# A Fourier mixing layer with a squared-ReLU FFN: the row d = 128 spread by DMA, its multiples made by GpSimd a block ahead, and squares taken in place

## The chip, the core and the metric

The kernel runs on one core of a Trainium2 chip. The metric is the device time of one execution in microseconds. One execution was also recorded by the hardware profiler; all durations of single instructions are from that one. In what follows PE is TensorE (PEld its weight loads), DVE is VectorE, ACT is ScalarE, POOL is GpSimd and SP is SyncE, and L763 is line 763 of the kernel.

## The reference

```python
# x (8, 3008, 256), w_in (256, 2048), w_out (2048, 256), all float32
y = np.fft.fft(np.fft.fft(x, axis=1), axis=2).real.astype(np.float32)
y = y.reshape(8 * 3008, 256)
h = np.maximum(y @ w_in, 0.0)
out = (h * h @ w_out).astype(np.float32)
```

The real part of a two-dimensional Fourier transform over 3008 positions and 256 channels replaces attention; a feed-forward layer with a squared ReLU follows.

## The kernel before, in words

**What is computed where.** The transform along the channels is folded into `w_in`: a table `gh` holds it in three forms (`gh[:, 0]` for cosines, `gh[:, 1]` for sines, `gh[:, 2]` for sines with a factor of minus two). The transform along the positions gives, for each column (one frequency k of one batch), a cosine part `zc` and a sine part `zs` of 128 channels each. With P the product of the cosine table with `zc` and Q that of the sine table with `zs`, one column serves two frequencies, k and S - k: one takes P + Q, the other P - Q. So the kernel goes over some 12,000 columns, not 24,064 rows, in 25 blocks (`wins`), 0 to 24: 240, 512, 512, 240, 512 and 448 columns, then 512 each, and 360 in the last.

**A block.** Each block `w` has eight steps `s`, and each step two chunks of 128 of the 2048 hidden channels. A normal step does the following.

- `pq` (L762, L763): four matmuls of up to 512 columns, into a PSUM tile `ph` (pool `ps_h`, two buffers).
- the square of the step before (`power`, L814, on VectorE), then the ReLU of the first sign (L809, on ScalarE) into a tile `h1`, and its square from `h1` into `h2`.
- `others`: the second product of the block before (`ffn2_steps`, L665, sixteen matmuls of 256 columns a step, so 128 a block), with its evacuation on ScalarE (L680) and its output stores on the SP queue (L645); the jobs of the folds of coming batches, on VectorE and GpSimd; and a share of the z matmuls (L558) that make `zc` and `zs` of the next block.
- `turn` (L798): two matmuls more, with `gh[:, 2]`, which turn P + Q into P - Q in the same PSUM tile.
- the ReLU of the second sign. Its square comes at the next step and reads `h1` backwards, since frequency S - k counts down.

A differencing step (steps 2, 4 and 6 of a block from block 4 on, or step 5 alone in a block with a fold, listed in `diff`) saves the two matmuls of `turn`. `cosines` (L784) makes P alone; `twice` (L788, VectorE) computes t2 = n2 - 2P from PSUM; after `others`, `sines` (L793) adds Q to the same PSUM tile, so it has to wait for `twice`; one ReLU is taken on ScalarE as ever, and the other on VectorE as a saturating add of t2 and P + Q (L807).

**The row d = 128.** Row 0 of `zs` carries the channel d = 128 in the place where the sine of d = 0 would be nought. `n2` is twice its contribution N: the row spread over all partitions times a column `g2n`. Before, `spread_nyq` spreads the row in step 0 of the same block by a matmul with `sel`, a matrix of ones in its first row (L770, into a tile of the pool `ps_z`), ScalarE takes it to `zn` (L772), and `nyq_rows` multiplies it on ScalarE, two instructions for each differencing step (L778).

**The order.** The schedule is manual: each engine executes its instructions in the order in which the code issues them, and SP and GpSimd their transfers likewise. `at[s]` and `post[s]` list the jobs of the folds for each step. Block `fold_at` does the first fold of a batch, block `late_at` its late part: two `fold8` (L472) and two `fold16` (L483) on VectorE, the last with `nyq8`, small copies on GpSimd (L489 to L491). The blocks with a first fold are 5, 8, 10, 13, 16 and 19 (one differencing step each); those with a late part 6, 9, 12, 15, 18 and 21. The z matmuls of the odd frequencies (unit `e = 0`) and of the even ones (`e = 1`, which read what the late part and `nyq8` wrote) are spread over the steps `lo` to `hi`; each unit has two parts, 0 for `zc` (cosine) and 1 for `zs` (sine), and two halves `h`. After the last matmul of a part, `minus` (L581, VectorE) writes the second run of its columns.

Of the kernel before, what the change touches and what calls it, by code (L numbers as in the profile page):

```python
# [16 lines left out]
P = 128  # L17
# [12 lines left out]
def kernel(  # L30
# [76 lines left out]
    h1p = ctx.enter_context(tc.tile_pool(name="h1p", bufs=3))  # L107
    h2p = ctx.enter_context(tc.tile_pool(name="h2p", bufs=2))
    wp = ctx.enter_context(tc.tile_pool(name="wp", bufs=2))
    znp = ctx.enter_context(tc.tile_pool(name="znp", bufs=1))  # L110
# [73 lines left out]
    sel = const.tile([P, P], F16, name="sel")  # L184
    nc.gpsimd.memset(sel, 0.0)
    nc.gpsimd.memset(sel[0:1, :], 1.0)
# [350 lines left out]

    def z_steps(u, late=False):
# [15 lines left out]
        def mm(part, h, k, last, o0, o1, lhs, tab):  # L554
            if h == 0 and k == 0:
                st[part] = ps_z.tile([P, 512], F32, name="pz", tag="pz")
# [21 lines left out]
        def minus(part):  # L578
            es, ps = st["es", part], st[part]
            for w, o, a, cnt in spans(c0 + n, n2):  # L580
                nc.vector.scalar_tensor_tensor(out=zwin(w)[part][:, o : o + cnt], in0=es[:, a : a + cnt], scalar=2.0, in1=ps[:, a : a + cnt], op0=ALU.mult, op1=ALU.subtract)  # L581
# [126 lines left out]
    diff = {w: (5,) if w in fold_at else (2, 4, 6) for w in range(4, NW)}  # L708
    BIG = 3.0e38
    old = None  # L710
    for w in range(NW):
# [4 lines left out]
        lo, hi = 0, NST - 1  # L716
# [48 lines left out]
        n2s = {}  # L765
        t2s = {}

        def spread_nyq():
            pn = ps_z.tile([P, 512], F32, name="pn", tag="pz")
            nc.tensor.matmul(pn[:, 0:wn], sel, zsw[:, 0:wn], start=True, stop=True)  # L770
# [3 lines left out]
        def nyq_rows(s):  # L774
            n2 = n2s[s] = wp.tile([P, 2, WN], F32, name="n2", tag="w16")
            for a in range(2):
                fc = 2 * s + a
                nc.scalar.activation(n2[:, a, 0:wn], n2s["zn"][:, 0:wn], AF.Copy, bias=0.0, scale=g2n[:, fc : fc + 1])  # L778
# [7 lines left out]
        def twice(s):  # L786
            t2 = t2s[s] = tmp.tile([P, 3 * NE], F32, name="t2", tag="tt")[:, 0 : 2 * WN].rearrange("p (a n) -> p a n", a=2)
            nc.vector.scalar_tensor_tensor(out=t2[:, :, 0:wn], in0=phs[s][:, :, 0:wn], scalar=-2.0, in1=n2s[s][:, :, 0:wn], op0=ALU.mult, op1=ALU.add)  # L788
# [11 lines left out]
        def relu(s, sg):  # L800
            h1 = h1p.tile([P, 2, 512], F16, name="h1", tag="h1")
            if w == 1 and not sg:

                for a in range(2):
                    nc.scalar.activation(h1[:, a, 0:wn], phs[s][:, a, 0:wn], AF.Relu, bias=0.0, scale=-1.0)
            elif sg and s in t2s:
                nc.vector._custom_dve(TENSOR_ADD_SAT, out=h1[:, :, 0:wn], in0=t2s[s][:, :, 0:wn], in1=phs[s][:, :, 0:wn], s0=BIG, s1=0.0)  # L807
            else:
                nc.scalar.activation(h1[:, :, 0:wn], phs[s][:, :, 0:wn], AF.Relu, bias=0.0, scale=-1.0)  # L809
            return h1  # L810

        def power(s, sg, h1):
            hv = rev_dim(h1[:, :, 0:wn], 2) if sg else h1[:, :, 0:wn]
            nc.vector.tensor_tensor(h2[:, 2 * s : 2 * s + 2, sg * wn : (sg + 1) * wn], hv, hv, op=ALU.mult)  # L814

        def square(s, sg):
            power(s, sg, relu(s, sg))
# [14 lines left out]
        kept = None  # L832
        for s0 in range(0, NST, 2 if w == 0 else 1):
            ss = range(s0, s0 + (2 if w == 0 else 1))
            if s0 in diff.get(w, ()):
                cosines(s0)
                twice(s0)
                if kept:
                    power(*kept)
                others(s0)  # L840
                sines(s0)
                h1a = relu(s0, 0)
                h1b = relu(s0, 1)
                power(s0, 0, h1a)
                kept = (s0, 1, h1b)
            else:
                for s in ss:
                    pq(s)
                if kept:
                    power(*kept)  # L850
                for s in ss:
                    square(s, 0)
                if s0 + 1 in diff.get(w, ()):
                    nyq_rows(s0 + 1)
                for s in ss:
                    others(s)
                if s0 == 0 and w in diff:
                    spread_nyq()
                for s in ss:
                    turn(s)  # L860
                if w == 0:
                    for s in ss:
                        square(s, 1)
                    kept = None
                else:
                    kept = (s0, 1, relu(s0, 1))
        if kept:
            power(*kept)
# [35 lines left out]
```

## Time and profile before

| what | value |
|---|---|
| median of 3 runs | 641.57 us (639.27 to 641.66) |
| the profiled execution's own time | 640.49 us |
| its span, first to last instruction | 638.5 us |
| mean granted TensorE clock | 0.994 |
| TensorE busy | 603.5 us, 95% of the span |
| ScalarE busy | 476.9 us, 75% |
| VectorE busy | 472.3 us, 74% |
| GpSimd busy | 75.9 us, 12% |

A row of a group reads: line, engine, operation, output <- input by the program's names, shapes, count, then the busy time in us, the mean of one in ns, and the idle time of the engine just before, with what ended it. A row of waits reads: engine and what waited <- what ended the wait, total us, times, longest. A row of the timeline reads: start in us, duration in us, engine, line, operation, what it writes <- what it reads, shapes, how many in a row. The ends of matmuls are modelled, and their durations overlap, so the distance from one start to the next says more than the duration.

### The profile page before, as it was taken

To read this page: it belongs to the slowest core of one execution; us is meant where nothing else is said; L and a number is where in the kernel's file an instruction comes from. 1 tells how busy PE (TensorE), PEld (TensorE's weight loads), DVE (VectorE), ACT (ScalarE), POOL (GpSimd) and SP (SyncE) were. 2 spreads that over 40 slices of the span, in tenths; PEclk is the share of its full clock that TensorE was granted. 3 is DMA by queue.
4 is the path that set the end of the run, shared out by engine and by line. 5 is a ranking of instruction groups with operands and counts; after the bars stand their busy time and mean duration, and the time that the engine had idled before them with its cause. 6 is when DMAs were issued, how large, how long until landed. Compare 5 with 4: busy or idle time off the path is not lost.

```text
span 638.5 us, 11636 instructions
## 1 busy us (share of the span) xinstructions
PE 603.5 (95%) x4485; PEld 431.5 (68%) x4485; DVE 472.3 (74%) x712; ACT 476.9 (75%) x690; POOL 75.9 (12%) x134
## 2 busy tenths in 40 slices
PE   4799998799999999999999999999999999999995
PEld 2456686576677766776667776777767766677784
DVE  7777855896969868768788578877788677787660
ACT  6677767877788777787868787778777877787761
POOL 8202220012000220220003200021000200000000
PEclk9989999999999999999999999999999999999998
DMA  8736331135111731631116411173111311111121
GB/s 152 111 84 126 110 87 43 32 73 158 45 43 35 147 109 34 122 114 54 35 51 120 122 33 49 39 147 96 45 28 56 107 37 38 45 45 49 39 61 55
DMA packets 36543, 47.53 MB, mean 74 GB/s; under 512 B 4232, under 2 KB 30344, under 8 KB 36488
## 3 DMA queue, kind: packets, MB, share of 16 engines
q0 software_dynamic: 9344, 22.14, 17.1%
q1 hardware_dynamic: 26915, 24.44, 12.8%
q8 instruction: 35, 0.57, 0.4%
q10 hardware_dynamic: 228, 0.21, 0.1%
q14 instruction: 21, 0.16, 0.1%
HBM read 33.63 MB, written 27.84 MB: 96 GB/s over the span
## 4 chain that ended last, share of the span: by engine, by line
PE 70%; DVE 15%; ACT 6%; issue 4%; POOL 2%; DMA 1%; ACTq 1%; POOLq 0%; DVEq 0%
PE po L665 38%; PE ph L763 7%; PE ph L762 7%; PE ph L798 7%; DVE h L814 4%; PE ph L793 4%; DVE t L788 4%; ACT h L809 3%; DVE h L807 3%; PE pz L558 3%; PE ph L784 2%; DVE xy L472 1%; ACTq L645 1%; POOL xo L133 1%; PE pn L770 1%
## 5 line engine op out<-in xcount | busy, mean ns | idle before, releaser
L809 ACT ACTIVATE h<-ph 128x1024 f16<-128x1024 f32 (+3 forms) x341 | 315.8, 970 | 73.2 <-PE ph L793 48.4
L665 PE MATMUL po<-wout,h 128*128 128x256 f16 (+1 forms) x3024 | 362.0, 273 | 0.0
L665 PEld LDWEIGHTS <-h 128*128 128x128 f16 (+1 forms) x3024 | 296.8, 98 | 72.0 <-issue 0.6
L814 DVE TENSOR_TENSOR h<-h 128x1024 f16<-128x1024 f16 (+3 forms) x400 | 251.9, 655 | 72.7 <-ACT h L809 67.0
L762 PE MATMUL ph<-zc,gh 128*128 128x512 f16 (+3 forms) x298 | 107.7, 365 | 2.7 <-ACT h L809 1.3
L763 PE MATMUL ph<-zs,gh 128*128 128x512 f16 (+3 forms) x298 | 107.7, 365 | 0.9 <-DVE zs L581 0.7
L807 DVE CUSTOM_DVE_ANT_0 h<-t,ph 128x1024 f16<-128x1024 f32 x47 | 57.4, 1221 | 44.5 <-ACT h L809 43.4
L798 PE MATMUL ph<-zs,gh 128*128 128x512 f16 (+3 forms) x298 | 83.9, 364 | 3.8 <-ACT h L809 2.2
L680 ACT ACTIVATE osb<-po 128x512 f32<-128x512 f32 (+2 forms) x94 | 54.9, 587 | 33.6 <-PE po L665 28.7
L788 DVE SCALAR_TENSOR_TENSOR t<-ph,n 128x1024 f32<-128x1024 f32 (+2 forms) x51 | 61.1, 1199 | 14.0 <-PE ph L784 11.0
L778 ACT ACTIVATE n<-zn,g2n 128x512 f32<-128x512 f16 (+2 forms) x102 | 67.3, 717 | 0.0
L763 PEld LDWEIGHTS <-gh 128*128 128x128 f16 x298 | 29.1, 98 | 34.6 <-issue 3.6
L762 PEld LDWEIGHTS <-gh 128*128 128x128 f16 x298 | 29.1, 98 | 32.4 <-issue 2.0
L793 PE MATMUL ph<-zs,gh 128*128 128x512 f16 (+2 forms) x102 | 29.8, 373 | 10.4 <-DVE t L788 9.8
L798 PEld LDWEIGHTS <-gh 128*128 128x128 f16 x298 | 27.9, 98 | 13.1 <-issue 6.2
L784 PE MATMUL ph<-zc,gh 128*128 128x512 f16 (+2 forms) x102 | 29.9, 375 | 0.0
L772 ACT ACTIVATE zn<-pn 128x512 f16<-128x512 f32 (+2 forms) x21 | 12.4, 589 | 17.7 <-PE pn L770 17.6
L489 POOL COPY xy<-xy 128x2 f16<-128x2 f16 x16 | 2.5, 188 | 164.8 <-DVE xy L472 164.8
L793 PEld LDWEIGHTS <-gh 128*128 128x128 f16 x102 | 9.4, 97 | 16.8 <-issue 14.3
L128 POOL DMA_DIRECT2D xo<-in_x_dram x8 | 6.1, 765 | 119.5 <-DVE fo L423 109.0
L133 POOL DMA_INDIRECT xo<-in_x_dram,idx_r x15 | 18.3, 1218 | 4.5 <-issue 4.3
L784 PEld LDWEIGHTS <-gh 128*128 128x128 f16 x102 | 10.0, 98 | 11.6
(134 smaller groups left out, 344.2 us busy)
## 6 DMA issues: line engine op xcount, KB each, us to landing
out_dram<-osb SPq DMA_DIRECT2D x77, 128.0 KB
xo<-in_x_dram POOLq DMA_DIRECT2D x7, 768.0 KB, 6.7
scr<-ev POOLq DMA_DIRECT2D x8, 390.0 KB, 3.3
rb<-scr POOLq DMA_DIRECT2D x16, 130.0 KB
out_dram<-osb SPq DMA_DIRECT2D x12, 94.0 KB
w<-in_moe_w_in_dram POOLq DMA_DIRECT2D x2, 512.0 KB
wout<-in_moe_w_out_dram POOLq DMA_DIRECT2D x1, 1024.0 KB
out_dram<-osb SPq DMA_DIRECT2D x8, 75.0 KB
```

Source lines behind the costliest of these rows:

```text
L665: nc.tensor.matmul(po[0:m, j * D : (j + 1) * D], h2[:, fc, q : q + m], wout16[:, fc, :], start=(fc == 0), stop=(fc == NFC - 1))
L680: nc.scalar.activation(osb[0:mm].rearrange("p s d -> p (s d)")[:, lo:hi], po[0:mm, lo:hi], AF.Copy, bias=0.0, scale=HS * HS)
L762: nc.tensor.matmul(ph[:, a, 0:wn], gh[:, 0, f0 : f0 + P], zcw[:, 0:wn], start=True, stop=False)
L763: nc.tensor.matmul(ph[:, a, 0:wn], gh[:, 1, f0 : f0 + P], zsw[:, 0:wn], start=False, stop=True)
L778: nc.scalar.activation(n2[:, a, 0:wn], n2s["zn"][:, 0:wn], AF.Copy, bias=0.0, scale=g2n[:, fc : fc + 1])
L784: nc.tensor.matmul(ph[:, a, 0:wn], gh[:, 0, f0 : f0 + P], zcw[:, 0:wn], start=True, stop=True)
L788: nc.vector.scalar_tensor_tensor(out=t2[:, :, 0:wn], in0=phs[s][:, :, 0:wn], scalar=-2.0, in1=n2s[s][:, :, 0:wn], op0=ALU.mult, op1=ALU.add)
L793: nc.tensor.matmul(phs[s][:, a, 0:wn], gh[:, 1, f0 : f0 + P], zsw[:, 0:wn], start=False, stop=True, skip_group_check=True)
L798: nc.tensor.matmul(phs[s][:, a, 0:wn], gh[:, 2, f0 : f0 + P], zsw[:, 0:wn], start=False, stop=True, skip_group_check=True)
L807: nc.vector._custom_dve(TENSOR_ADD_SAT, out=h1[:, :, 0:wn], in0=t2s[s][:, :, 0:wn], in1=phs[s][:, :, 0:wn], s0=BIG, s1=0.0)
L809: nc.scalar.activation(h1[:, :, 0:wn], phs[s][:, :, 0:wn], AF.Relu, bias=0.0, scale=-1.0)
L814: nc.vector.tensor_tensor(h2[:, 2 * s : 2 * s + 2, sg * wn : (sg + 1) * wn], hv, hv, op=ALU.mult)
```

## The change

- The row of the next block's `zs` is written by SP to a row of DRAM and read back into all 128 partitions (`zn`), in step 6 of the block before (step 7 where the z matmuls end late). The matmul with `sel` and its copy on ScalarE go, and so does `sel`.
- The products `n2` for all differencing steps of the next block are made at once after that, on GpSimd. The pool of `n2` has three buffers, that of `zn` two.
- The ReLUs write straight into `h2`, the one of the second sign backwards; `h1` goes. One in-place square for each step, over both signs, comes one step later (after `twice`, where that next step is a differencing one); step 7's first sign is squared at once.
- The z matmuls end a step earlier in general (`hi`), and take part 1 before part 0. `minus` of a step that stands ahead of a differencing step is held until after `twice`.
- Fold jobs move: `odds` to step 5, and the late jobs to steps 2, 4, 6 and 7. Block 4 has two differencing steps, not three.

```diff
+    held = {"on": False, "jobs": []}
+    def let_go():
+        jobs, held["jobs"] = held["jobs"], []
+        for j in jobs:
+            j()
...
         def minus(part):
+            if held["on"]:
+                held["jobs"].append(lambda: apart(part))
+            else:
+                apart(part)
...
-    diff = {w: (5,) if w in fold_at else (2, 4, 6) for w in range(4, NW)}
+    diff = {w: (4, 6) if w == 4 else (5,) if w in fold_at else (2, 4, 6) for w in range(4, NW)}
...
-        lo, hi = 0, NST - 1
+        lo, hi = 0, NST - 2
...
-            at = [[f] for f in fj[0:5]] + [[], fj[6:7], fj[7:8]]
-            post[5] = fj[5:6]
+            at = [[f] for f in fj[0:4]] + [[], fj[4:5], fj[6:7], fj[7:8]]
+            post[6] = fj[5:6]
...
-                at[st + 2] = at[st + 2] + folds[late_at[w]]["late"][st : st + 1]
+                at[(2, 4, 6, 7)[st]] += folds[late_at[w]]["late"][st : st + 1]
...
-            zj += [(zu, 0, 0), (zu, 1, 0), (zu, 0, 1), (zu, 1, 1)]
+            zj += [(zu, 1, 0), (zu, 0, 0), (zu, 1, 1), (zu, 0, 1)]
...
         def spread_nyq():
-            pn = ps_z.tile([P, 512], F32, name="pn", tag="pz")
-            nc.tensor.matmul(pn[:, 0:wn], sel, zsw[:, 0:wn], start=True, stop=True)
-            zn = n2s["zn"] = znp.tile([P, WN], F16, name="zn", tag="zn")
-            nc.scalar.activation(zn[:, 0:wn], pn[:, 0:wn], AF.Copy, bias=0.0, scale=1.0)
...
-                nc.scalar.activation(n2[:, a, 0:wn], n2s["zn"][:, 0:wn], AF.Copy, bias=0.0, scale=g2n[:, fc : fc + 1])
+            wn1 = wins[w + 1][1]
+            row = drp.tile([1, WN], F16, name="row", tag="row")
+            nc.sync.dma_start(out=row[:, 0:wn1], in_=zwin(w + 1)[1][0:1, 0:wn1])
+            zn = znp.tile([P, WN], F16, name="zn", tag="zn")
+            nc.sync.dma_start(out=zn[:, 0:wn1], in_=bass.AP(tensor=row.tensor, offset=row.offset, ap=[[0, P], [1, wn1]]))
+            for s in diff[w + 1]:
+                n2 = n2s[w + 1, s] = wp.tile([P, 2, WN], F32, name="n2", tag="w16")
+                for a in range(2):
+                    fc = 2 * s + a
+                    nc.gpsimd.tensor_scalar(out=n2[:, a, 0:wn1], in0=zn[:, 0:wn1], scalar1=g2n[:, fc : fc + 1], scalar2=None, op0=ALU.mult)
...
         def relu(s, sg):
-            h1 = h1p.tile([P, 2, 512], F16, name="h1", tag="h1")
+            h = h2[:, 2 * s : 2 * s + 2, sg * wn : (sg + 1) * wn]
+            if sg:
+                h = rev_dim(h, 2)
...
-        def power(s, sg, h1):
-            hv = rev_dim(h1[:, :, 0:wn], 2) if sg else h1[:, :, 0:wn]
-            nc.vector.tensor_tensor(h2[:, 2 * s : 2 * s + 2, sg * wn : (sg + 1) * wn], hv, hv, op=ALU.mult)
+        def power(s, a, b):
+            h = h2[:, 2 * s : 2 * s + 2, a * wn : b * wn]
+            nc.vector.tensor_tensor(h, h, h, op=ALU.mult)
...
+            held["on"] = s0 + ng in diff.get(w, ())
             if s0 in diff.get(w, ()):
                 cosines(s0)
                 twice(s0)
-                if kept:
-                    power(*kept)
+                settle()
                 others(s0)
                 sines(s0)
-                h1a = relu(s0, 0)
-                h1b = relu(s0, 1)
-                power(s0, 0, h1a)
-                kept = (s0, 1, h1b)
+                relu(s0, 0)
+                relu(s0, 1)
+                kept.append((s0, 0, 2))
+                if s0 == hi and w + 1 in diff:
+                    spread_nyq()
+                continue
```

`settle` takes the squares that are kept and then calls `let_go`; in a normal step it comes right after `pq`.

More of the change, by code (lines that the diff above doesn't have):

```diff
@@ L578, in minus, with apart @@
         def minus(part):
+            if held["on"]:
+                held["jobs"].append(lambda: apart(part))
+            else:
+                apart(part)
+        def apart(part):
             es, ps = st["es", part], st[part]
@@ L830, in others, with settle @@
                     j()
-        kept = None
-        for s0 in range(0, NST, 2 if w == 0 else 1):
-            ss = range(s0, s0 + (2 if w == 0 else 1))
+        kept = []
+        def settle():
+            for k in kept:
+                power(*k)
+            kept.clear()
+            let_go()
+        ng = 2 if w == 0 else 1
+        for s0 in range(0, NST, ng):
+            ss = range(s0, s0 + ng)
+            held["on"] = s0 + ng in diff.get(w, ())
             if s0 in diff.get(w, ()):
```

65 lines of the change are left out of this document (25 added, 40 removed).

## The prediction

> **What bounds the kernel now.** I read the busy shares first, then the waits of TensorE, then the order in time of one block of 512 columns, and last the few GpSimd rows there are.
>
> ```profile
> span 638.5 us, 11636 instructions
> PE 603.5 (95%) x4485; PEld 431.5 (68%) x4485; DVE 472.3 (74%) x712; ACT 476.9 (75%) x690; POOL 75.9 (12%) x134
> PE ph L793 <- DVE t L788: 9.8, 15, 1.7
> L770 PE MATMUL pn<-zs,sel 128*128 128x512 f16 x19 | 7.2, 379 | 0.0
> ```
>
> TensorE is the bound; only work taken from it, or a wait of it that ends, moves the time. A matmul's 379 ns overlap with the next. By starts, a 512-column matmul comes every 216 ns (300.30, 300.52, 300.73 in the timeline) and a 256-column one every 109 ns. Its largest wait is L793, the sines of a differencing step, behind L788 (`twice`). Two such steps, columns start, duration, engine, line:
>
> ```profile
> 306.60 0.59 PE L784 MATMUL ph<-zc,gh 128*128 128x512 f16 x2
> 307.30 1.23 DVE L788 SCALAR_TENSOR_TENSOR t<-ph,n 128x1024 f32<-128x1024 f32 x1 [0.82 <-PE ph L784]
> 308.78 0.59 PE L793 MATMUL ph<-zs,gh 128*128 128x512 f16 x2
> ...
> 311.61 1.89 DVE L814 TENSOR_TENSOR h<-h 128x1024 f16<-128x1024 f16 x3
> 312.25 0.59 PE L784 MATMUL ph<-zc,gh 128*128 128x512 f16 x2
> 313.41 0.69 DVE L472 TENSOR_TENSOR xy<-rb 128x1040 f16<-128x1040 f16 x1
> 314.02 1.22 DVE L788 SCALAR_TENSOR_TENSOR t<-ph,n 128x1024 f32<-128x1024 f32 x1
> 315.29 0.59 PE L793 MATMUL ph<-zs,gh 128*128 128x512 f16 x2 [0.70 <-DVE t L788]
> ```
>
> In the first, VectorE is free, `twice` starts 0.70 us after the cosines, and the sines follow the sixteen output matmuls without a hole. In the second, three squares and a fold job stand ahead of it: it starts 1.77 us after the cosines, 1.07 late, and the sines stop for 0.86 (0.25 us or less of lateness costs nothing). Over the run, by starts, the sines stop in 25 places, 14.4 us together (the 9.8 above counts idle from a modelled end). Each of the 25 has VectorE busy right up to `twice`.
>
> The GpSimd rows that price what is added:
>
> ```profile
> L159 POOL IOTA irow_i<- 128x377 int32 x1 | 0.5, 483 | 0.0
> L183 POOL TENSOR_SCALAR perm<-prow_i 128x128 f16<-128x128 int32 x2 | 1.7, 840 | 0.1
> L489 POOL COPY xy<-xy 128x2 f16<-128x2 f16 x16 | 2.5, 188 | 164.8 <-DVE xy L472 164.8
> 12.40 1.76 DVE L395 TENSOR_TENSOR u<-xo 128x3072 f16<-128x3072 f16 x1
> 12.55 1.71 POOL L221 TENSOR_SCALAR evs<-evec 128x2 f32<-128x2 f32 x1
> scr<-ev POOLq DMA_DIRECT2D x8, 390.0 KB, 3.3
> ```
>
> A two-column GpSimd instruction, 0.19 us elsewhere, took 1.71 and ended 0.1 us after the VectorE TENSOR_TENSOR beside it: the two shut each other out.
>
> **The change, part by part.** The sum is made against the profiled execution's 640.49 us (span 638.5 and 2.0 around it); the median of the runs is 641.57, 1.1 above.
>
> *Matmuls.* The 21 spreading matmuls go: 19 x 0.216 + 0.19 + 0.15 = 4.45 us, all on the bound. Block 4 loses its differencing step 2, so four matmuls become six there: +0.43.
>
> *ScalarE* loses 21 x 0.59 (L772) and 102 x 0.717 (L778) = 80 us. It is not the bound, so this counts nothing directly. ReLUs of the second sign now write backwards; no row shows that on ScalarE. VectorE's backward reads cost nothing (squares of both directions lie at 0.68 to 0.69), so I take nought. A doubled write would add about 1 us to some 150 ReLUs, 40 us where ScalarE then binds; I give it no more than the tail of the range.
>
> *Squares.* 1024 elements take 687 ns and 3072 (L419) 1786, so 0.537 ns each; one of 2048 takes 1.24 us, 0.14 less than two. More matters that the square of a step's first sign no longer runs one step early. Ahead of `twice` stood three squares (2.06 us), now one: 0.82 sooner. The xy jobs (0.69, 0.42) and `odds` (0.97) move from the step before a differencing step into it, behind `twice`, and the z subtractions of L581 (0.3 to 0.5) are held until after it. The lateness of 1.07 above meets 0.82 + 0.69, and that of 0.64 in the fold blocks meets 0.97. Only block 4 keeps an xy job ahead. So the 14.4 us go. What is late next is the second ReLU (L807) behind these moved jobs: 1.22 `twice` + 1.24 square + 0.69 xy, so it starts 3.1 us after `twice` where the sines allow 2.2, ends at 4.4, and its square at 5.6. The next `twice` comes after 3.04 + 2.61 = 5.65 (six or four matmuls of 0.216 with sixteen of 0.109). That is just enough, and not everywhere: I leave 1.5 us (bounds 0 and 7).
>
> *The row by DMA.* Two transfers on SP, the second behind the first, are queued behind the output stores of step 5, and the step-7 stores wait behind them. Those have three buffers and 6 us between stores, so nobody waits. Step 5's output matmuls end 16.95 us into a block (three steps of 3.04, two of 2.61, then 0.86 + 1.75); the stores are issued 0.95 to 2.0 us later (by the starts around 325); the row goes at 18.95. Its two landings are bounded by 0.85 each (issue to first packet in the trace's packets) and 3.3 each (`scr`); 2.3 each, nearer the second since one engine may still hold store packets, gives the row at 23.6.
>
> *2N on GpSimd.* 50 steps x 2 = 100 instructions of 512 columns. Lower bound: IOTA's slope, (483 - 167)/371 = 0.85 ns a column, gives 0.60 us. Upper: from COPY to `perm`, (840 - 188)/126 = 5.2 ns a column, gives 2.8 us. I take 0.8, near the lower end, because both `perm` ran beside VectorE instructions with two SBUF inputs, which the 1.71 us row shows to lengthen them; with 0.15 of such waiting, 0.95 each. [...] `twice` of step 2 needs its pair 6 us after the row, so up to 3 us an instruction this is hidden.
>
> *What is queued behind it.* GpSimd runs in order. In the late-fold blocks the copies of `nyq8` (L489 to L491) now come in step 7, behind these instructions. And because the pass over P comes first, the first z matmul of the following block reads what they write. It stands after L762/L763 and sixteen output matmuls: 23.03 (block length) + 0.86 + 1.75 = 25.7. The copies end at 23.6 + n x 0.95 + 0.4. In blocks 6 and 21 n is 6 (the next block has three differencing steps): 29.7, a stop of 4.0 us each. In blocks 9, 12, 15 and 18 n is 2: 25.9, a stop of 0.2 each. Together 8.8 us; with c the price of one instruction, 20c - 10.2 once both kinds stop.
>
> Sum: 640.49 - 4.45 + 0.43 - 14.4 + 1.5 + 8.8 = 632.4, and 1.1 for the median: 633.5.
>
> **The rivals.**
>
> *GpSimd slower than I take it* (ends slower). The same stop at the first z matmul grows by 20 us for each microsecond of c; from c = 1.36 it has eaten all the rest (20 x 1.36 - 10.2 = 16.9). At c = 2.0, in the middle of the bounds with its waits, it is 29.8 us: 640.5 - 16.9 + 29.8 + 1.1 = 654.5. For it speaks the `perm` row, against it IOTA and that overlap. Chance 0.15; at c = 1.6 it is 646.5.
>
> *No stop.* The row lands by 22.4 and c is near 0.6: the copies are in time but for 1 us or so: 640.49 - 18.4 + 0.5 + 1.1 + 1.1 = 624.8. The edge of 623 has none at all. Chance 0.17.
>
> [...] A square and a GpSimd instruction exclude each other, as L395 and L221 did, now the other way round: a square waits a whole GpSimd instruction. Most fall in steps 7 to 1, where VectorE has one square of 1.24 in 3.04 us and nothing urgent. If instead, in each of the 14 blocks with three differencing steps, one held `twice` back by 0.8 less the free 0.25, it were 14 x 0.55 = 7.7 us more: 641.2. Chance 0.1. [...]
>
> *The sines go on waiting.* If the moved jobs and the late L807 cost the full 7 instead of 1.5 us: 639.0. Chance 0.08. That the row does not arrive by step 2 (a `twice` waiting for n) needs 3 us an instruction and lies beyond the second bound.
>
> **The numbers.** My case has the remaining 0.5, its own range 627 to 639. The range 623 to 648 leaves out the dearer GpSimd and the backward writes. What a measurement of this kernel can tell from no change is about 0.5%, 3.2 us: 638.4 to 644.8. Faster: 0.5 less a twentieth, 0.17, and some of the two cases at 639 and 641, 0.67. Within: 0.14. Slower: 0.19, nearly all of it the dear GpSimd.
>
> **What would show it.** Right: no L770; the wait of the sines for `twice` under 2 us; no square pair but one of 2048 elements near 1.24; the GpSimd multiply near 0.8 to 1.0; TensorE stops for the `nyq8` copies at the first z matmul of blocks 7 and 22, some 4 us each; ScalarE busy near 397. Wrong: a multiply over 1.4, TensorE waiting behind `twice` with VectorE idle before it (n late), or ScalarE's ReLU over 1.1 us. No stop in blocks 7 and 22 would make the time some 8 us less.

## The result, and the profile after

The changed kernel takes 731.0 us (median of 4 runs, 728.96 to 734.67) beside 640.87 for the kernel before: a ratio of 1.1416, 95% interval 1.1362 to 1.147. The forecast was 633.5 with a range of 623 to 648. The profiled execution took 728.96 us, its span is 727.2, and the mean granted clock fell from 0.994 to 0.945.

From the page: the span, TensorE's busy time, and the chain that ended last, by engine.

```profile
span 727.2 us, 11242 instructions
...
PE 613.9 (84%) x4466; PEld 434.5 (60%) x4466; DVE 461.8 (64%) x535; ACT 414.1 (57%) x568; POOL 258.7 (36%) x232
...
PE 57%; DMA 14%; POOL 9%; ACT 6%; DVE 5%; SPq 4%; issue 3%; POOLq 0%; ACTq 0%; DVEq 0%
```

TensorE is still the bound, but for 84% of the span instead of 95. DMA and GpSimd, which were to stay off the path, carry 23% of the chain. What TensorE waited for (total us, times, longest):

```profile
PE pz L562 <- POOL xy L485: 49.4, 6, 13.2
PE ph L803 <- DVE t L798: 23.8, 7, 9.1
PE ph L794 <- DVE h L819: 17.9, 2, 9.2
```

The first is the stop at the first z matmul that the prediction named. The second is the sines behind `twice`, the wait that was to go. The third is new. (The lines of the changed kernel: L562 z matmuls, L773/L774 `pq`, L794 cosines, L798 `twice`, L803 sines, L819 the second ReLU on VectorE, L821 the ReLUs on ScalarE, L825 squares, L788 the multiplies, L781/L783 the two transfers of the row, L808 `turn`, L452 the transfers of `rb`, L655 the output stores, L468 `fold8`, L485 to L487 `nyq8`.) Each of the three is followed back in the trace in turn.

**The first z matmul.** Block 21 is undisturbed until its end. It begins at 604.9. SyncE's queue, then GpSimd's, then TensorE's, around its end:

```profile
624.47 1.36 SPq L781 DMA_DIRECT2D row<-zs  x1
631.35 0.35 SPq L783 DMA_DIRECT2D zn<-row  x1
```

```profile
634.46 9.27 POOL L788 TENSOR_SCALAR n<-zn,g2n 128x512 f32<-128x512 f16 x6 [18.45 <-DMA zn<-row]
643.67 0.31 POOL L485 COPY xy<-xy 128x2 f16<-128x2 f16 x2
```

```profile
643.92 0.34 PE L562 MATMUL pz<-sin,xy 128*128 128x188 f16 x1 [13.21 <-POOL xy L485]
...
645.14 0.63 PE L773 MATMUL ph<-zc,gh 128*128 128x512 f16 x1
645.57 0.63 PE L774 MATMUL ph<-zs,gh 128*128 128x512 f16 x1
```

The row is issued 19.6 us into the block (forecast 18.95). The broadcast can be issued only when the row is in DRAM, 6.9 us later, and the first multiply starts 3.1 after that (forecast 2.3 and 2.3). Six multiplies take 9.3 (forecast 5.7), and only then come the copies that the z matmul reads. The stop is 13.2 instead of 4.0: the copies end 0.6 + 5.4 + 3.6 us later than forecast. The first z matmuls of blocks 7, 10, 13, 16 and 19 stop as well, for 12.5, 2.8, 4.8, 4.8 and 12.2 us by the starts; the forecast had 4.0 for block 7 and 0.2 for the other four, which have two multiplies each. After the stop above, the matmuls start 0.43 us apart, not 0.216: TensorE runs at half its rate, and its granted clock from 640 to 647 us is 0.50.

**The cosines.** GpSimd and VectorE at the change from block 5 to block 6 (145.9):

```profile
151.69 10.02 POOL L788 TENSOR_SCALAR n<-zn,g2n 128x512 f32<-128x512 f16 x6 [6.27 <-DMA zn<-row]
161.66 1.16 POOL L452 DMA_DIRECT2D rb<-scr  x2
```

```profile
167.35 0.70 DVE L468 TENSOR_TENSOR xy<-rb 128x1040 f16<-128x1040 f16 x1 [10.15 <-DMA rb<-scr,idx_r]
167.97 1.22 DVE L819 CUSTOM_DVE_ANT_0 h<-t,ph 128x1024 f16<-128x1024 f32 x1
```

The transfers that fetch `rb` for `fold8` stand behind the six multiplies in GpSimd's queue. `fold8` therefore waits on VectorE, the second ReLU (L819) waits behind `fold8` though its own inputs are there, and the cosines, which need its PSUM buffer, stop for 9.2 us. The same happens in block 9.

**The sines.** In blocks 11 and 17 above all (8.1 and 9.3 us) `twice` waits for n. Before block 11 (309.1) the row was issued only at 311.93, since five of the eight output stores ahead of it on SP took 1.9 to 3.9 us each to issue between 297 and 312, against a median of 0.35. Meanwhile GpSimd's loads of x kept the DMA engines full: their busy tenths in 40 slices from 295 to 312 us, and the sines of block 11:

```profile
DMA  0009278999999999999999951216000052886000
```

```profile
326.41 1.01 PE L803 MATMUL ph<-zs,gh 128*128 128x512 f16 x2 [7.96 <-DVE t L798]
```

What the row itself waits for can be read from the packets. In step 6 of block 17 it is issued at 510.78, right behind output stores of 61 and 67 KB, and the broadcast only at 518.38. SyncE's queue, and what the DMA engines moved between 513 and 518 us:

```profile
510.78 2.11 SPq L781 DMA_DIRECT2D row<-zs  x1
518.38 0.35 SPq L783 DMA_DIRECT2D zn<-row  x1
...
DMA packets 117, 0.12 MB, mean 23 GB/s; under 512 B 3, under 2 KB 117, under 8 KB 117
...
q1 hardware_dynamic: 117, 0.12, 6.6%
```

All but three of these packets are of 1 KB, the size of an output row. They follow one another every 0.042 us and take 6.6% of the time of the 16 DMA engines, about that of one; nothing else moves. The row is the last of the train: its own packet starts 7.0 us after its issue. Twelve of the 13 rows that took 3.4 us or more end such a train; in y2 below, where two rows have no packet ahead of them, they take 1.1 us. So the row stands behind the rows of the stores ahead of it. This is read from the packets; no run changed the stores.

Summed by the starts of the matmuls from 126 us on (the blocks with the row), the z matmuls stop for 50.5 us, the sines 23.7, the cosines 18.2, and matmuls at half rate behind such stops (119 gaps) lose 16.8: 109.2 together. Less the stops of before in the same part, 10.9, less 3.9 of streaming (the matmuls that go), less 3.0 in the part ahead of 126 us and 3.2 at the two ends, that is 88.2 of the 88.7 us by which the span grew.

The groups with each shape apart (busy us, mean ns of one | idle before):

```profile
L788 POOL TENSOR_SCALAR n<-zn,g2n 128x512 f32<-128x512 f16 x92 | 166.5, 1822 | 256.3 <-DMA zn<-row 248.9 <-DVE h L825 7.4
...
L825 DVE TENSOR_TENSOR h<-h 128x2048 f16<-128x2048 f16 x147 | 181.7, 1236 | 118.1 <-ACT h L821 115.5 <-issue 0.9
...
L821 ACT ACTIVATE h<-ph 128x1024 f16<-128x1024 f32 x282 | 277.6, 1024 | 157.9 <-PE ph L808 90.5 <-PE ph L803 58.7 <-PE ph L774 6.5
```

A multiply is 1.82 us on the mean; one with VectorE quiet is 1.56 (six in 9.27 above), and the longest is 3.07. The merged square is at its price of 1.24, and a ReLU costs what it did with those of the second sign writing backwards (1024 ns on the mean; 1027 before).

### The profile page after: what moved, and what is told of

It reads as the page before. It is cut to its first block, busy times and chain, and to the rows that moved or that the text cites. A ratio compares the mean times of both kernels' runs of the same rounds, so it can differ in the third digit from the quotient of the medians.

```text
span 727.2 us, 11242 instructions
## 1 busy us (share of the span) xinstructions
PE 613.9 (84%) x4466; PEld 434.5 (60%) x4466; DVE 461.8 (64%) x535; ACT 414.1 (57%) x568; POOL 258.7 (36%) x232
## 4 chain that ended last, share of the span: by engine, by line
PE 57%; DMA 14%; POOL 9%; ACT 6%; DVE 5%; SPq 4%; issue 3%; POOLq 0%; ACTq 0%; DVEq 0%
PE po L675 32%; DMA row<-zs 8%; POOL n L788 7%; PE ph L808 6%; PE ph L773 6%; PE ph L774 6%; DMA zn<-row 5%; SPq L655 4%; ACT h L821 3%; PE pz L562 3%; PE ph L803 2%; PE ph L794 2%; DVE t L798 2%; DVE h L819 1%; DVE h L825 1%
## 5 line engine op out<-in xcount | busy, mean ns | idle before, releaser
L821 ACT ACTIVATE h<-ph 128x1024 f16<-128x1024 f32 (+3 forms) x342 | 316.7, 968 | 174.0 <-PE ph L808 100.1
L675 PE MATMUL po<-wout,h 128*128 128x256 f16 (+1 forms) x3024 | 366.9, 275 | 0.0
L825 DVE TENSOR_TENSOR h<-h 128x2048 f16<-128x2048 f16 (+7 forms) x225 | 236.6, 1063 | 136.8 <-ACT h L821 131.5
L788 POOL TENSOR_SCALAR n<-zn,g2n 128x512 f32<-128x512 f16 (+2 forms) x100 | 178.8, 1800 | 277.2 <-DMA zn<-row 269.8
L773 PE MATMUL ph<-zc,gh 128*128 128x512 f16 (+3 forms) x300 | 111.6, 375 | 5.4 <-DVE zc L591 2.2
L774 PE MATMUL ph<-zs,gh 128*128 128x512 f16 (+3 forms) x300 | 111.4, 375 | 0.0
L798 DVE SCALAR_TENSOR_TENSOR t<-ph,n 128x1024 f32<-128x1024 f32 (+2 forms) x50 | 60.1, 1202 | 62.5 <-POOL n L788 34.4
L808 PE MATMUL ph<-zs,gh 128*128 128x512 f16 (+3 forms) x300 | 86.5, 372 | 3.6 <-ACT h L817 1.9
L819 DVE CUSTOM_DVE_ANT_0 h<-t,ph 128x1024 f16<-128x1024 f32 x46 | 56.1, 1220 | 17.8 <-ACT h L821 16.8
L562 PE MATMUL pz<-sin,xy 128*128 128x188 f16 (+1 forms) x64 | 13.6, 239 | 49.4 <-POOL xy L485 49.4
L774 PEld LDWEIGHTS <-gh 128*128 128x128 f16 x300 | 30.1, 100 | 40.3 <-issue 11.9
L803 PE MATMUL ph<-zs,gh 128*128 128x512 f16 (+2 forms) x100 | 30.9, 392 | 23.8 <-DVE t L798 23.8
L773 PEld LDWEIGHTS <-gh 128*128 128x128 f16 x300 | 30.1, 100 | 33.6 <-issue 4.4
L794 PE MATMUL ph<-zc,gh 128*128 128x512 f16 (+2 forms) x100 | 30.1, 384 | 17.9 <-DVE h L819 17.9
L562 PEld LDWEIGHTS <-xy 128*128 128x128 f16 x128 | 11.3, 100 | 51.9 <-POOL xy L485 51.1
L808 PEld LDWEIGHTS <-gh 128*128 128x128 f16 x300 | 27.5, 99 | 11.5 <-issue 6.1
L444 POOL DMA_DIRECT2D scr<-ev x8 | 4.8, 596 | 67.0 <-DVE od L437 50.3
L794 PEld LDWEIGHTS <-gh 128*128 128x128 f16 x100 | 9.8, 98 | 29.6 <-issue 18.4
L803 PEld LDWEIGHTS <-gh 128*128 128x128 f16 x100 | 9.5, 100 | 27.7 <-issue 25.8
L468 DVE TENSOR_TENSOR xy<-rb 128x1040 f16<-128x1040 f16 x16 | 11.0, 694 | 20.4 <-DMA rb<-scr,idx_r 20.4
```

Source lines behind the costliest of these rows:

```text
L675: nc.tensor.matmul(po[0:m, j * D : (j + 1) * D], h2[:, fc, q : q + m], wout16[:, fc, :], start=(fc == 0), stop=(fc == NFC - 1))
L773: nc.tensor.matmul(ph[:, a, 0:wn], gh[:, 0, f0 : f0 + P], zcw[:, 0:wn], start=True, stop=False)
L774: nc.tensor.matmul(ph[:, a, 0:wn], gh[:, 1, f0 : f0 + P], zsw[:, 0:wn], start=False, stop=True)
L788: nc.gpsimd.tensor_scalar(out=n2[:, a, 0:wn1], in0=zn[:, 0:wn1], scalar1=g2n[:, fc : fc + 1], scalar2=None, op0=ALU.mult)
L794: nc.tensor.matmul(ph[:, a, 0:wn], gh[:, 0, f0 : f0 + P], zcw[:, 0:wn], start=True, stop=True)
L803: nc.tensor.matmul(phs[s][:, a, 0:wn], gh[:, 1, f0 : f0 + P], zsw[:, 0:wn], start=False, stop=True, skip_group_check=True)
```

## The experiments

Three theories were on the table. *Queue*: the multiplies cost nothing by themselves; what costs is where they and the two transfers stand in SP's and GpSimd's queues, ahead of work that TensorE soon needs and behind transfers that are late. *Row*: the late row alone. *Shut-out*: multiplies on GpSimd slow VectorE wherever they run. The expectations call them Q, R and P (once M); their S is that the new order of squares and fold jobs costs time by itself. Each run is compared with runs of the kernel before on the same chip; ratios have 95% intervals.

### The change without the row on GpSimd (x1)

```diff
 # against the changed kernel: the row as before the change, in its own block
-            nc.sync.dma_start(out=row...) ; nc.sync.dma_start(out=zn...) ; nc.gpsimd.tensor_scalar(...)
+            nc.tensor.matmul(pn[:, 0:wn], sel, zsw[:, 0:wn], start=True, stop=True)
+            nc.scalar.activation(zn[:, 0:wn], pn[:, 0:wn], AF.Copy, bias=0.0, scale=1.0)
+            # and nyq_rows(s0 + 1) on ScalarE, a step ahead
```

> The change without its row: the matmul with the ones row, the copy and the 2N multiplies stay on TensorE and ScalarE in the block itself, as before; squares in place, held subtractions, moved fold jobs, pass over P first and block 4's two differencing steps are as in the change. Theory Q (the loss is all in the row and in GpSimd's queue, the rest is the gain I forecast): 640.9 - 14.4 + 1.5 + 0.4 = 628 us, no wait of the sines for twice over 2 us in total, no wait of the z matmuls for the nyq8 copies. Theory S (the new order of squares and fold jobs costs time by itself): over 650. Theory P (GpSimd shuts out the squares): 628 as well.

Measured: 625.21 us, ratio 0.9775 [0.9758, 0.9791]. The wait of the sines in its trace:

```profile
PE ph L806 <- DVE t L801: 1.2, 3, 0.6
```

Everything else in the change gains 15 us, and does it where the prediction put it: the sines' wait falls from 9.8 to 1.2. The whole loss, 106 us against this kernel, belongs to the row and its multiplies. S falls.

### The fold jobs in their old steps (y5)

```diff
 # against x1
-            at = [[f] for f in fj[0:4]] + [[], fj[4:5], fj[6:7], fj[7:8]]
-            post[6] = fj[5:6]
+            at = [[f] for f in fj[0:5]] + [[], fj[6:7], fj[7:8]]
+            post[5] = fj[5:6]
...
-                at[(2, 4, 6, 7)[st]] += folds[late_at[w]]["late"][st : st + 1]
+                at[st + 2] += folds[late_at[w]]["late"][st : st + 1]
```

> The squares alone, with the fold jobs back in their old steps (odds in step 4, the late jobs in steps 2 to 5): what moving them is worth. By the sum of the prediction the lateness of twice was 1.07 us in the late blocks, of which one square instead of three takes 0.82 and 0.25 is free, and 0.64 in the fold blocks: 625 to 626. If the moves carry the gain, the five blocks with 0.86 + 0.59 come back: 630 to 633.

Measured: 626.53 us, 0.9795 [0.9778, 0.9811]; the sines wait 1.8 us in all. That is half a microsecond above the first reading and far below the second. Moving the jobs is worth at most 1.3 us of the 15; the two intervals overlap, so even that is not shown. Nearly all of the gain is in what both kernels have, the merged square that is no longer ahead of `twice` and the held subtractions among it; no run takes these apart.

### The row by DMA, the multiplies on ScalarE (x2)

```diff
 # against the changed kernel: the transfers stay, the multiplies go back
-                    nc.gpsimd.tensor_scalar(out=n2[:, a, 0:wn1], ...)      # a block ahead
+                nc.scalar.activation(n2[:, a, 0:wn], n2s["zn"][:, 0:wn], AF.Copy, ...)   # own block
```

> The change with the 2N multiplies on ScalarE, a step ahead in the block itself; the row still goes through DRAM in the block before. Theory Q in the form that GpSimd's queue alone is at fault: 624 to 630 us. In the form that the two transfers are late as well: ScalarE then stands in step 1 and waits for the row, in the blocks where the row comes after the block's start by more than 4 us (11, 17, 20 and 23 by the row issues of the changed kernel), 3 to 8 us each: 640 to 660. Theory P: 628. Theory S: 680 or more.

Measured: 639.43 us, 0.9995 [0.9984, 1.0006]. Waits of TensorE, and of ScalarE:

```profile
PE ph L804 <- DVE t L799: 14.6, 7, 6.8
...
ACT n L789 <- DMA zn<-row: 17.8, 5, 8.1
```

The late row by itself eats 14 us against x1: in blocks 11 and 17, where the sines stop for 6.1 and 7.0 us, it lands after step 2 has begun, with no GpSimd multiply anywhere. The time is just under the 640 to 660 expected of late transfers. So the row is late by its transfers, not by the multiplies.

### The transfers ahead of step 5's stores (y2)

```diff
 # against x2: spread_nyq() one step earlier, before others(s)
+                if s0 == hi - 1 and w + 1 in diff:
+                    spread_nyq()
                 others(s0)
...
-                if s0 == hi and w + 1 in diff:
-                    spread_nyq()
```

> As the row by DMA with the multiplies on ScalarE, but the two transfers are issued on SP ahead of step 5's output stores instead of behind them (step 5 instead of step 6; blocks 3 and 4 as before). Theory Q with the stores as the cause of the late row: the row comes 3 to 4 us earlier, more where the stores themselves were slow; the 14.6 us that the sines waited mostly go: 622 to 627 us, below the 625.2 of the squares alone, since 4.4 us of matmuls go as well. If the late row comes from its own transfers (the write of one row landing after 1.3 to 7.6 us), 3 us earlier only: 630 to 636.

Measured: 622.68 us, 0.9734 [0.9718, 0.9751]; the sines wait 1.2 us. One place in SP's queue is worth 17 us here. The row is as slow to land as before (1.1 to 8.4 us), but it starts earlier, and behind no output store of step 5.

### The row by matmul, the multiplies on GpSimd (x3)

```diff
 # against the changed kernel: no transfers, the row by matmul in the block before
-            nc.sync.dma_start(out=row[:, 0:wn1], in_=zwin(w + 1)[1][0:1, 0:wn1])
-            nc.sync.dma_start(out=zn[:, 0:wn1], in_=...)
+            nc.tensor.matmul(pn[:, 0:wn1], sel, zwin(w + 1)[1][:, 0:wn1], start=True, stop=True)
+            nc.scalar.activation(zn[:, 0:wn1], pn[:, 0:wn1], AF.Copy, bias=0.0, scale=1.0)
```

> The change with the row spread by a matmul and a ScalarE copy in step 6 or 7 of the block before; the 2N multiplies stay on GpSimd, a block ahead. Their start is then about 21 us into the block, free of the SP queue. Theory Q: six multiplies of 1.56 to 1.9 us end at 31 to 32 us, the first z matmul wants the nyq8 copies at 25.7, so 6 us in blocks 7 and 22 and none where there are two multiplies; the rb transfers of blocks 5 and 8 come late by 2 to 5 us: 628 + 4 + 12 + 6 = 650. If the wait for the transfers made most of the stops, 640 to 655; if the multiplies alone made them, 700 or more. Theory P: 700 or more too, with squares of 2048 elements well over 1.24 us.

Measured: 662.57 us, 1.0357 [1.0335, 1.0378]. Waits of TensorE:

```profile
PE ph L797 <- DVE h L822: 12.6, 2, 6.3
PE pz L565 <- POOL xy L488: 12.1, 2, 6.1
```

That is 8 us above the 640 to 655 expected of Queue, and well below the 700 of Shut-out. With the row in time, the kernel still loses 37 us against x1: by the two stops of the changed kernel, each smaller, by some 10 us of matmuls at half rate behind them (its granted clock is 0.979), which the expectation did not count, and by 4.2 us in which two spreading matmuls wait for `zs`. Neither the row nor the queue of GpSimd alone is the 106; together they are more than their sum (14 + 37), because everything behind the multiplies also waits for the row that they wait for.

### Multiplies nobody reads (y3)

```diff
 # against x1: 100 multiplies more on GpSimd, from step 3 on, into a tile that is never read
-    wp = ctx.enter_context(tc.tile_pool(name="wp", bufs=3))
+    wp = ctx.enter_context(tc.tile_pool(name="wp", bufs=2))      # n2: room for spare
...
+            if s0 == 3 and w in diff:
+                for s in diff[w]:
+                    for a in range(2):
+                        nc.gpsimd.tensor_scalar(out=spare[:, a, 0:wn], in0=n2s["zn"][:, 0:wn], ...)
```

> [...] Theory P: each multiply holds up a square for up to 1.56 us: 630 to 650. Theory Q: the multiply gives way and the square does not: 625 to 627, multiplies of 1.8 us on average, squares of 2048 elements within 2% of 1.223 us.

Measured: 625.83 us, 0.9783 [0.9767, 0.98], the same as x1. Its squares:

```profile
L829 DVE TENSOR_TENSOR h<-h 128x2048 f16<-128x2048 f16 x147 | 185.7, 1263 | 67.4 <-ACT h L825 65.7
```

A hundred multiplies in the middle of the blocks lengthen the squares by 40 ns each (1223 in x1), 3% where at most 2% was expected, and cost no time. The multiplies lengthen more, to 1.93 us on the mean (1.56 with VectorE quiet). So Shut-out falls for multiplies at this place; whether the work is as cheap a block ahead, beside other squares, is left to z4.

### All multiplies at the end of the block (x4, y1)

```diff
 # x4, against the changed kernel; y1 is the same on x3
-            for s in diff[w + 1]:          # in spread_nyq, step 6 or 7
+        def multiply():
+            for s in diff[w + 1]:
...
+        if w + 1 in diff:                  # after the last step's jobs
+            multiply()
```

> The change with the GpSimd multiplies issued at the very end of the block, behind the rb transfers and the nyq8 copies, and nothing else altered (row by DMA, same place). Theory Q: the waits of the z matmuls for the copies (49.4 us) and of the fold jobs for rb (20.4 us, of which 18 on TensorE) go; the waits of twice for a late n (23.8 on TensorE) stay: 731 - 49 - 18 = 664, less some 8 us of matmuls at half clock behind the stops: 655 to 664. Theory P: 700 to 731, since the same multiplies run beside the same squares. Theory S: 710 or more.

> Both repairs of the row at once, the 2N multiplies still on GpSimd: the row spread by a matmul and a ScalarE copy in step 6 or 7 of the block before, and the multiplies issued at the end of that block, behind the rb transfers and the nyq8 copies. Theory Q (only lateness and queue order cost): no wait for the copies, for rb or for n is left; 625.2, the time of the squares alone, plus up to 3 for the two spreading matmuls of blocks 3 and 4 that wait for zs: 625 to 630 us. Theory P (the multiplies themselves cost, by the squares that they hold up): 640 or more. If it comes to about 640, GpSimd's multiplies are still too slow for step 2 in some blocks, and twice waits for n there.

Measured: x4 665.05 us, 1.0383 [1.0349, 1.0417], a microsecond above Queue's range; y1 650.48, 1.0161 [1.0142, 1.0181]. In x4 the stops for the copies and for `rb` are gone, and the sines wait 35.8 us for n instead. y1 was expected near x1 and missed; by its time alone it falls to Shut-out, which had 640 or more. Waits of TensorE and of GpSimd in y1:

```profile
PE ph L809 <- DVE t L804: 18.9, 9, 5.3
...
POOL rb L455 <- DMA scr<-ev: 27.1, 7, 6.7
```

I had overlooked that the `rb` transfers themselves wait in GpSimd's queue for a scratch row to land. In the six blocks after a fold the multiplies now stand behind that wait. A fixed place at the end only swaps one wait for another.

### The transfers early, the multiplies left in place (z1)

```diff
 # against the changed kernel: only the two transfers of the row one step earlier
+                if s0 == hi - 1 and w + 1 in diff:
+                    spread_nyq()           # row and zn, ahead of step 5's stores
                 others(s0)
...
                 if s0 == hi and w + 1 in diff:
-                    spread_nyq()
+                    multiply(diff[w + 1])
```

> The changed kernel, with its two transfers of the row (and nothing else) issued one step earlier on SP, ahead of step 5's output stores; the multiplies stay where the change has them on GpSimd. Theory Q (the loss is the order of GpSimd's queue: copies of nyq8 and the rb transfer behind the multiplies, plus the lateness of the row): the row's lateness goes, the queue behind six multiplies stays. Six multiplies of 1.8 us from about 3 us after an earlier landing end some 14 us after it, so the rb wait of VectorE and the first z matmul still stop TensorE, though by some 5 us less each: as x3 (matmul spread, multiplies on GpSimd), 655 to 670. Theory R (the row's lateness alone is the loss): 625 to 632. Theory M (the multiplies themselves slow VectorE or ScalarE): 700 or more, since they are all still there.

Measured: 667.58 us, 1.0436 [1.0413, 1.0459], in Queue's range. Waits of TensorE:

```profile
PE ph L797 <- DVE h L822: 16.2, 2, 9.2
PE pz L562 <- POOL xy L485: 16.0, 3, 6.3
```

63 us of the loss go with the lateness of the row, and what stays are the two stops behind the six multiplies, as in x3.

### The first pair alone ahead (z2)

```diff
 # against z1
-                    multiply(diff[w + 1])
+                    multiply(diff[w + 1][:1])
...
+        if w + 1 in diff:
+            multiply(diff[w + 1][1:])      # end of the block
```

> As z1, and of the multiplies only the first differencing step's pair stays where it was; the other pairs (two or four instructions) are issued at the end of the block, behind the rb transfer and the copies of nyq8. All operations of the change are kept, on the same engines; only their order in the two queues differs. Theory Q (queue order and lateness are the whole loss): two instructions ahead of the copies and of rb cost under 4 us and end before anyone waits, the later pairs are needed 5 and 10 us after the first: 622 to 628, as the squares alone (625.2) or the row before the stores with ScalarE multiplying (622.7). If the multiplies on GpSimd cost by themselves (its traffic beside VectorE): 640 or more. If the pairs at the end still stand behind an rb transfer that waits for the scratch row, as in y1: 630 to 640, with twice waiting for n in the blocks after a fold block.

Measured: 644.78 us, 1.0067 [1.0043, 1.009], above the 622 to 628 of Queue, and again where the expectation put multiplies that cost by themselves (640 or more). The trace shows stops instead: 8.7 us of the sines for n, 5.8 for `rb` and 4.6 for the copies. GpSimd at the change to block 6, which still loses 7.5 us:

```profile
150.31 3.77 POOL L791 TENSOR_SCALAR n<-zn,g2n 128x512 f32<-128x512 f16 x2 [4.88 <-DMA zn<-row]
154.04 1.16 POOL L452 DMA_DIRECT2D rb<-scr  x2
```

The row took 8.7 us to DRAM there, beside a fold's transfers. Even a pair holds up `rb` if it waits for its input: here `rb` paid not only the 3.8 us of the pair's work but its 4.9 us of wait as well.

### ScalarE where a fold came before (z3), and two orders mended (z4)

```diff
 # z3, against z2: the blocks after a fold multiply on ScalarE, in their own block
+            if w in fold_at:
+                return                     # in multiply()
+            if w - 1 in fold_at and s0 + 1 in diff.get(w, ()):
+                nyq_rows(s0 + 1)
 # z4, against z3: nyq_rows before others(s), and a fold block's own pair at the end
+        nf = 0 if w + 1 in fold_at else 1
-                multiply(diff[w + 1][:1])  ...  multiply(diff[w + 1][1:])
+                multiply(diff[w + 1][:nf])  ...  multiply(diff[w + 1][nf:])
```

> As z2, and in the six blocks that follow a block with a fold (6, 9, 11, 14, 17 and 20) the pairs are multiplied by ScalarE, in their own block, as before the change; the other 15 blocks keep GpSimd. In z2 the blocks that are still longer than before are 6, 11, 14, 17, 19 and 22, by 7.5, 4.7, 0.6, 2.9, 5.8 and 0.1 us, and all but the last have to do with a row that lands late during a fold's transfers and with the pair of multiplies that waits for it ahead of the rb transfer or of the copies. Theory Q (what is left of the loss is that pair's place in GpSimd's queue in those six blocks): 621 to 626. If GpSimd's multiplies cost something by themselves wherever they run: 632 or more, since 70 of the 100 stay.

> As z3, with two orders mended: the pair of multiplies for a block with a fold is issued at the end of the block before it, behind the copies of nyq8 (z3 stopped 4.6 us at 477 us there), and ScalarE's multiplies of the six blocks stand ahead of that step's output copies instead of behind them (z3: ten stops of the sines, 6.9 us). 70 of the 100 multiplies stay on GpSimd, a block ahead. Theory Q (order is all): 635.6 less 4.6 and 6.9, and a little of the slow clock behind the long stop, 622 to 626. If GpSimd's multiplies cost by themselves: 630 or more.

Measured: z3 635.6 us, 0.9926 [0.9909, 0.9943], 10 us above Queue's range and in the range of the rival (632 or more); its two remaining waits:

```profile
PE ph L814 <- DVE t L809: 6.4, 13, 0.7
PE pz L562 <- POOL xy L485: 4.6, 1, 4.6
```

Both are orders again: ScalarE's multiplies stood behind output copies that wait for matmuls, and the pair for block 19 stood ahead of the copies of `nyq8`. z4 mends these two places and takes 620.45 us, 0.9693 [0.9669, 0.9718]: a little below Queue's range, far from the 630 of the rival, and the lowest time here (its interval touches that of y2). From its page:

```profile
span 618.5 us, 11256 instructions
...
PE 595.3 (96%) x4466; PEld 429.2 (69%) x4466; DVE 464.4 (75%) x535; ACT 432.8 (70%) x604; POOL 204.7 (33%) x196
...
L800 POOL TENSOR_SCALAR n<-zn,g2n 128x512 f32<-128x512 f16 (+2 forms) x64 | 122.5, 1925 | 146.1 <-DMA zn<-row 116.2
```

Sixty-four multiplies are left on GpSimd (the expectations say 70, a miscount), each slower than in the changed kernel (1925 against 1800 ns), and the sines wait 1.1 us in all (1.2 in x1 and y2). That settles it between Queue and the rival: sixty-four multiplies a block ahead on GpSimd cost no time that can be measured where nobody is queued behind them. The other 36 run on ScalarE here; no run has all hundred on GpSimd, with their results used, and no stop.

### The order of the two passes (y4)

```diff
 # against the changed kernel
-            zj += [(zu, 1, 0), (zu, 0, 0), (zu, 1, 1), (zu, 0, 1)]
+            zj += [(zu, 0, 0), (zu, 1, 0), (zu, 0, 1), (zu, 1, 1)]
```

> The changed kernel, with the pass over P put back behind the other pass, as it was before the change. The first z matmul of a block then reads the other half, and the one that reads the copies of nyq8 comes one job later, 1 to 3 us into the block. If the order of the passes is what makes the copies' lateness a stop, the 49.4 us at the first z matmul goes: about 680. If lateness is so long (13 us) that any order meets it: each of the six stops shrinks by 3 us at most, 713 to 722. The rb waits and the late n stay either way.

Measured: 707.96 us, 1.1058 [1.1, 1.1116], between the two readings and near the second. The stops at the z matmuls shrink by 2.0 to 3.4 us each (13.4 to 10.0 at the last), 16 us in all, and about 19 come back in the profiled executions, 23 by the medians. So the new order of the passes makes the copies' lateness dearer, as the prediction said, but it is a fifth to a quarter of the loss.

## Why the prediction was wrong, step by step

**Right.** *Matmuls*: forecast -4.0, streaming fell by 3.9. *Squares and the sines' stops*: forecast -14.4 + 1.5 (and 0.4 for block 4), so 12.5; x1 gained 15.0, and the other 2.5 were not followed up; the sines are left 1.2. The merged square cost 1.24 and the backward ReLU nothing, as taken. ScalarE's busy time was forecast at 397 and is 414. The two products of that working come to 85.5, not 80, and the durations did fall by that; but in the profile neighbours overlap, so the busy time fell by 62.8. ScalarE is not the bound. The mechanism that was to cost, the first z matmul behind the copies of `nyq8`, is the largest wait of the profile after.

**The multiply.** Forecast 0.8 and 0.15 of waiting; it is 1.56 alone and 1.82 on the mean. I took a value near the lower end of 0.60 to 2.8, by IOTA, which reads no tensor. The truth lay in the middle of my own bounds. My reason for the low end, that both `perm` ran beside VectorE instructions with two SBUF inputs, was misread: the second ran almost wholly beside a TENSOR_SCALAR with one input (9.54 to 10.56) and was no shorter (853 ns after 826). Yet even with c at 1.82 my formula 20c - 10.2 gives 26.2 us, and the stop is 50.5. The rival of the slower GpSimd had the mechanism and the sign, and by its own working only some 651 us; the multiply is not the main fault.

**The row at 23.6 us.** This is the step that failed first. I bounded a landing by 0.85 and 3.3 and took 2.3. Measured, the first transfer took 1.3 to 7.6 us and the first multiply began 3.0 to 3.4 after the second was issued (more in a few blocks); undisturbed blocks had it between 24.7 and 29.6 us. The `scr` row that I used as the upper bound was a median, 3.3, and a bound from a median is none. That an engine may still hold store packets was the right thought, and 2.3 was the wrong size: the stores ahead held the row for up to some 6 us more. I also gave the stores ahead of it 0.95 to 2.0 us by one place in the trace. In the trace of before, 17 of the 312 stores take over 1 us to issue, up to 5.5; none of them lies near the place at 325 us that I read. So the prediction's last rival, a `twice` waiting for n, put beyond the second bound, came true at ordinary prices of the multiply: x2 has that wait with the multiplies on ScalarE. In block 18 the row is issued 28.5 us into the block, and two multiplies are enough for the 12.2 us by which block 19 stops.

**What is queued behind it.** I looked for who stands behind the multiplies and found the copies, but passed over the `rb` transfers, whose issue is also GpSimd's work. They cost 18.2 us in two blocks. And I priced an instruction that waits at its duration: its wait for the row goes to everybody behind it too. That is why the late row costs 14 us with ScalarE multiplying (x2 against x1) and, by the runs after and z1, 63 with GpSimd.

**The half rate.** Not priced: 16.8 us in 119 gaps. In the changed kernel each stop of 4.75 to 13.4 us is followed by matmuls of 512 columns 0.43 us apart, at a price of 1.3 to 2.8 us, and the stops of 1.5 to 3.1 us by next to none; elsewhere it is 0.216. The granted clock at the half rate is 0.50 (640 to 647 us in the changed kernel). y2 and z4, which have no such stop, have none of it from 126 us on, and their mean clocks are 0.998 and 0.999. Behind z3's only long stop, 4.75 us, there are nine such gaps, 1.4 us. But half rate also followed stops of 2.2 us in x4 (486 us) and 2.4 us in z2 (296 us; its granted clock is down to 0.8 in the slice from 289 to 305 us). So the length of a stop alone does not tell the stops with half rate from those without here, and what else does is not shown. From the stops of 4.75 us I estimate that the forecast's two stops of 4.0 should have carried 1.4 to 2.8 us more each.

**The squares beside the multiplies.** The rival in which a square waits a whole GpSimd instruction put 7.7 us on it and is refuted by y3 and z4. The pair of rows that it rested on shows only the GpSimd instruction lengthened: the VectorE one beside it took 1.76 us for its 3072 elements, no more than the 1.79 of L419. In y3 both kinds lengthen beside each other, the squares by 40 ns (1223 to 1263) and the multiplies by some 0.37 us (1.56 to 1.93), and since the multiplies have slack wherever nobody waits behind them, the price was nought.

## What to carry to other kernels

Before work goes to an idle engine, list what already passes through its queue, transfers that it issues included, and ask for each who is waiting for it and when; an instruction put ahead of them cost them its duration and its own wait here (3.8 and 4.9 us for `rb` in z2). A transfer's price is read from the worst rows in the stage where it will run, not from a median over the run, and with what stands ahead of it in its own queue. Nearly the same operations in another order took 731 or 620 us here (the latter with 36 of the 100 multiplies on ScalarE).

## What the runs showed of the hardware

- A GpSimd multiply of a 128x512 row by a column, f16 to f32, took 1.56 us with VectorE quiet, 1.82 on the mean of the changed kernel, and 3.07 at the longest, beside VectorE's work. With a hundred of them in the middle of the blocks a square of 2048 elements took 1263 ns (y3) against 1223 (x1).
- A row of 1 KB to DRAM took 1.1 us with no packet ahead of it (y2) and 1.3 to 7.6 us in the changed kernel, the long ones behind output stores whose 1 KB packets came one every 0.042 us (23 GB/s from 513 to 518 us), with nothing else under way. Beside a fold's loads it took up to 8.7 us (z2).
- While GpSimd's loads of x filled the DMA engines (297 to 312 us), single stores took 1.9 to 3.9 us to issue on SP, against a median of 0.35.
- Matmuls of 512 columns started 0.43 instead of 0.216 us apart for 2 to 5 us behind every stop of 4.75 us or more in the changed kernel, at a granted clock of 0.50 (640 to 647 us), and behind two of 2.2 and 2.4 us in x4 and z2; the mean clock of the changed kernel fell to 0.945.
- ScalarE's ReLUs of 1024 elements took 1024 ns on the mean with those of the second sign writing backwards, against 1027 before, with all forwards.
